# P transposed two chunks at a time, output stored two chunks at a time, and the ninth tokens moved in fewer transfers

## The chip, the cores and the metric

The kernel runs on one core of one Trainium2 chip. The metric is the device time of one execution in microseconds, lower is better. A core has five engines that run beside each other and wait for each other through semaphores: TensorE (PE in the profile, its weight loads are PEld), VectorE (DVE), ScalarE (ACT), GpSimd (POOL) and SyncE (SP), which does no arithmetic here and issues the DMA transfers. The inputs lie in the memory of the chip, are brought into the on-chip memory (128 partitions) by DMA, and TensorE writes its results into PSUM, from which DVE and ACT read.

## What is computed

Attention with a threshold over 8 batches, 8 heads, 576 tokens and 64 features a head, and behind it a feed-forward block with a maximum over three hidden layers:

```python
scores = scale * np.matmul(q, k.transpose(0, 1, 3, 2))
thresh = np.max(scores, axis=-1, keepdims=True) - tau
scores = np.where(scores >= thresh, scores, -1000000000.0)
scores = scores - np.max(scores, axis=-1, keepdims=True)
attn = np.exp(scores)
attn = attn / (np.sum(attn, axis=-1, keepdims=True) + 1e-09)
attn_out = np.matmul(attn, v)
x = attn_out.transpose(0, 2, 1, 3).reshape(B * S, H * D)      # 4608 x 512
h = np.maximum(np.maximum(x @ w1, x @ w2), x @ w3)            # 4608 x 768
out = h @ w_out                                               # 4608 x 512
```

## The kernel before

A "quad" is four heads of one batch, so there are 16 quads, two to a batch. Inside a quad the four heads are two couples, numbered r = 0 and 1, each of two heads, i = 0 and 1. The 576 tokens of a head are taken as 64 rows of nine tokens. Tokens 0 to 7 of each row make four blocks of 128 tokens; the last tokens of the 64 rows, the "ninth tokens", are a half block of 64. A quad has nine **chunks** of 128 query rows: four of i = 0 (numbers 0 to 3), one made of the ninth tokens of both i (number 4), four of i = 1 (numbers 5 to 8). There are 144 chunks in all.

For each chunk and each r TensorE makes a score tile of 128x576 in PSUM (`scores`), DVE takes its maximum (`maximum`), and the threshold and the exponentials are done in one of two ways, chosen by the table `MASKED`: by two passes on ACT, or by one on ACT and one on DVE (`exponents`, `numerators`). DVE takes the reciprocals of the sums for both r at once, and POOL multiplies and writes bf16 (`normalized`, lines 391 to 398): P, 128 x 1152, the two r beside each other. SP issues a transposing DMA (`turned`, lines 400 to 404) that writes P transposed into the tile `ptq` of the quad: nine blocks of 128 keys, and in each the columns of the chunk. There are six buffers for P (`PBUFS = 6`), so POOL can write P of chunk n only when the transfer of chunk n - 6 has landed.

When a quad is through, TensorE multiplies ptq with v (`product`), DVE and ACT copy the result to `xt`; with both quads of a batch done come the hidden layers (18 pieces a batch, `hid`), whose maximum is written to a tile `hT` of the batch (two buffers), and then the output: two pieces of two chunks each (`outp`) and one for the ninth tokens (`ninth`). ACT copies each output chunk from PSUM into a tile `ob` (four buffers) and SP stores it; the ninth tokens of a batch go out by two transfers. Batch 7 is split in two parts.

Loads, per quad: q and k (512 KB each), the ninth tokens of q and of k (64 KB each), v in two transfers, and the ninth tokens of v in two (`load`, lines 185 to 237). POOL casts v to bf16 (`cast_v`). All loads but three, all transposes and all stores but one are issued by SP.

The order is written out by hand in the string `ORDER`, one letter for each step, and `issue` carries it out. An engine does its steps in the order of the string. A capital is TensorE work and is followed by the number of the PSUM slot it writes (four slots of two banks): S a score tile, T the transposing of q and k on TensorE, O a product with v, F and B the two halves of a hidden or output piece, N a ninth piece. m, s, e, n, k and r are the steps of the softmax, p is half a P (POOL), t a transposing DMA (SP), l a load (SP), o and i stores (SP), y the casts of v, q a copy that swaps halves (POOL), and a, c, h, v, u, x, w and j are copies out of PSUM by ACT or DVE.

Before the first load lands, TensorE gets 12 transposes of the identity (`WARM = 12`, lines 607 to 609).

Every instruction of the kernel is recorded at line 93, a helper that keeps the order, so the profile's groups are told apart by tile names, not by lines.

Of the kernel before, what the change touches and what calls it, by code (L numbers as in the profile page):

```python
# [31 lines left out]
WARM = 12  # L32
# [3 lines left out]
PBUFS = 6  # L36
# [4 lines left out]
lllllllgllT0laclT1qqS0lacllzlqqS1mS2mS3lekS0lmlT1emlemalT2qclqkS1ylS3mgrlennemayS0elpcrS3nmpS1lnmplS2emT3gqq  # L41
esmtpS1erkT2paT0slceS3lpaT2ntS0cyqemS2ynrmtmqmqleenkS2plnS3resT1pmeS0qtmnpnpemzrteS2eznT3mpS0rcepaS3mytnqS1m
pT2lerapS3mgnS0plS2nqlermtpnmS3pntpermpS1mptekqT0mS2teeenkqnS3mrepmS1zcS0pmertenepS2mnpT1nmS3trS2mpS0enpmleg
yrmnplkeplS3ktS2eeknS0arrmptnS1mpmptS3mpS2eeremeS0ptmnS1ymnperkeptS3mT2encpS1lnsyO0mtqnmerkpgelnO2wqlnkpllS3
xrrreS0mptS2mnpT1maptesS2peS3pmteT1S0mpnS2cyS3lmO1lrmptmS0qewO2qennesrmepkS1epxkS3emF2nF0zmBkBpgT3ehnrF1vS2a
psS0nmzF3emBpgBesrrvS0tphS2mepF3mnT1plT0sBctapS2nvyF1nS0rsmtyT3eBzmeS2vpgS0mlpS1mF2lyennsqsmF0etBqrceBkpF1ht
S3snsvBnprF2vleS0pmBnpF1mhS3zsesrS0mS2epgmBntpF3ssvnF0qrBeqlF1evlzBemtBpS3hS2pnmS0tnrmO3pnmplnrsF2svgzeF0weB
pgS1evtyS3emBpS2nmtS1hkT3O0rakptmS3xrpsmS2ntpsS0smeF1pmT3etBqmnF2zvT0BtaczS1nvS3erlsmS2peS0lmpeS1mF3etmessF2
knlknlBkelresrmpS0npBmuptussrS1puS3umpS0lemS2lqeT1mtO3qnmqnssO0lpwelrncplS2xS1ptmeF0eF3mS2nokBetmF1hBrkpF2es
rBvnBpsevS3ytS0hmpS1emS2yepF3meF0trsmBpeBsvpnS2lnF1ymlT3nBvytaF2kT0hBkeF1lsrrecF3pBnvqBkF0phS2veS3mnptBmnpT2  # L50
F1sassrrlS3vpeS2lmepBlmF0eyoyS3vnoS2mnpBtsS1mphF3meT0tS2cF1ernsmBptS0esvpF2esmBqeS3lvqS0ntmqT1eBmyaF3rkF0hpB
nkS2nrsS1rvnBpmS3eptmO2pressmnptN1vepS3sweS0ptmjS2npmF1ekteT0knBrmpnssceT3yS2pasrrS0mqtuS3umpS2nmS0qleS1mlqe
S3ssmpS2oeO0ponmepmO1etqmerkO3pntkxrwS2xS0plmS3plmS1F2lpeeessmlnktT0eF3meBsscnlklnBkF0luF1rhktpBurBevF2pelS3
vpS0nlmByelmT1S3hlpsrsS0atmS2pnrS1mpeF3mtF0pemBnqF2ssvtnT1yBpecBqnrtS3vpnS1mS0hpmeF3tsmS1eBssrmepS0lrS2nvylF
1pemF3lyemBlBnskpoF2hsvT0oeBsprtS3avS1pnmF0eqS2tmF3epmBeqrS1stsvepS2mBepF0mlhT1nBkoO3nvtescS2nwT1nmF0F3akT2n
sBrrcpnBvS1phS2rmpetF3mepS0S1espmtS2epmBeF0rssmptT1eBkpaN2knO1snvjqtvS3xS2ermpS1nsS3rpmnS0mpteF2mpemqlnT1S3c
qnlS0rsqtmeS1BpmepmS0ektF1eemnklO3erslpulO0ynwlpnrklyS3xtrBskupermS0upS2umF3ptemS1pnS0mBnplsmS2hplF1meT3lBak
lF2ersqS3ovS0ntmpS1emBpeF3ssstvF0eBmeS2ktBhkF1nF3vniBmeBrF0sevpS2hrrspS1mnS3ptmeS2pmeF1qBstmeBpvnF2psS3snlrv
BylnmT1tS0hcpS3nmS2yepoF1rmeF0pomBeplF3ssvnBtyynBvT1hS2klaT0F3ssectqS1meS0qBrempT2eO1pmestaO0wnsrkpS2xvS1nF0
rpmnF3mptnBBsrpevS1phtS2meF0qsrS3mnpS1nmF2ptemBpT3esvT1qBtacS0eqS1rveqN3smepS2mnS0psmjS1ntmT2nF3cerlmpeS0klS  # L60
1peS2oknBlmnlrsmepO0lsuspkteO1uwelrS3kxlpS0emtF1empmF2oBktenekBkuS3hrsrS0pmuF2peS1smnpS3tmF0nysBmpeT1ryrtBsv
ayF3evS1pnS2mS0pemBpteS1mF2hpssmS0elF3emBlekBlF0nskF1tnsrBvpBhvyS2lpnvS0nqtS3rmepF1mF2eplBsmeBtrnrvS3pT0hmqF
1lnT2cBaT3knF0qvF2eBsqrceS1pvnBS3pstrmhS0pemS2nS1pmlF3nplsmF0eopBmS2oespsvS1ntBmeT3mO2atknsrsseF1vpS3terwpBn
mS0pS2hirmqS3nmS1qetF0smpF2nBpmetBpveS1S3rsempS0tnvpO1nsrmptesmS2peS3mxtF0meknT1oknS3S2lrecpBemyplermS1putS3
meF2ysmulykT1plN3akelO0kljesosO1weqtknqS3nrS0mleBpoxpmleT3S1cuF0nsorrF3mpnBtkpBhsS1uvS0lepS2meF3ymplF1eBsmle
BtsveS2F0hmF3nktBnT2kF1arBsvpnBrpveS0S2hptmS3nprF1smeS0plmF2nyisBmeF3vpBelsrBrqtvT1hT0qcS2epS3tmnS1ymapS2nsm
lS3peF0tsmpF1esmF2nBlrspnBrsovBnqtS3vhpS0empS2leF1mpS3lemBtnrmF0pF2nsvpBetsT3vBeS1rcepF0tkhO3ynmynrS2wnT1pmB
apT3tsssesT2cqN1avqeS3rS2jpmeF0pmtS1eBqnmS2qnsvS3S1qemS0pnmF2ntrkpesT3smBepmnrtcS1puS0umpS3erS2mtpeS1mpF0nsm
ekS3nS2meBkemnO1rupupmO3txskeO2ewtkS1rrpS3mS0pmptexnF2S1essmeBpmeF3F0tshkF1nrkS2peBlmBnlyssBvpF2ihvyF3eBssro
eS0pvBoepmO2teyvS0S1sremptF3wmpS0nS2nmoBmS1ihS0rmepF3tnF2pmBnkF0noBsrvpnBtS1vphS3sesmF0teF2mBerBpveS3ynF1yvp  # L70
F0nmS2tnBmBessF3khF2errvBpeBpvO0nkptO3hkN1wxsS2jeS0pmeS1tmF2srF3mepBrespBveS1ptS0vnpS2mnF3tnmrmF1peskepBerkn
ptBupoO2tO0xuO2wukuN3xrF1npF2hprF0vF1ptvF2hF0jpvF1vF2thF0vF1vF2hiF0vF1vF2ihF0vF1vF2ohF0voO1voO2wF0xF2F1hF3vF
2vF1hF3vF2vF1hF3vF2vF1hF3vF2vF1hF3vF2vF1hF3vBvF3uuoBoN0ufojdi
# [31 lines left out]
def kernel(  # L105
# [39 lines left out]
    wo = one.tile([128, NF, DM], BF16, name="wo")  # L145

# [38 lines left out]
    def load(g, first=False):  # L185
        b, qd = quads[g]
        L = Ls[g] = dict(b=b, qd=qd, first=first)
        for n in "qk":

            L[n] = ld.tile([128, 20, D], F32, name=n + "m")  # L190
        L["vm"] = ld.tile([128, 4, 4, D], F32, name="vm")
        L["vr"] = ld.tile([128, 2, D], F32, name="vr")

        def rows_of(src):
            return src[b, 4 * qd:4 * qd + 4].rearrange("(r i) (p c) d -> (i p) r c d", r=2, c=9)

        def both(n, src, rows, i=None):

            t = L[n].rearrange("p (r c) d -> p r c d", r=2)[rows, :, 0:8]
            return t, one_of(src, i)[:, :, 0:8] if i is not None else rows_of(src)[:, :, 0:8]  # L200
# [4 lines left out]
        if first:  # L205
            for i in range(2):
                put = [(n, src, half(n, i), nc.scalar if n == "k" and i == 0 else sync) for n, src in (("k", k), ("q", q))]
                for n, src, rows, e in put:
                    e.dma_start(out=L[n][rows, 8:10], in_=one_of(src, i)[:, :, 8])
                    yield  # L210
# [4 lines left out]
                for n, src, rows, e in put:  # L215
                    if i == 0:
                        e.dma_start(out=L[n][rows, 10:18], in_=one_of(src, i)[:, 1, 0:8])
# [24 lines left out]
    def cast_v(L):  # L242
# [4 lines left out]
        for r in range(2):  # L247
            rows = slice(64 * r, 64 * r + 64)
            pool.tensor_copy(out=L["vrb"][rows, 2 * r:2 * r + 2], in_=L["vr"][rows])
            yield  # L250
# [6 lines left out]
    def couple(L, n, r, j, rows=slice(0, 128)):  # L257

        f = 8 if j == 4 else 10 * r + (0, 4, 2, 6)[j]
        return L[n][rows, f:f + 2, :].rearrange("p a d -> p (a d)")  # L260
# [25 lines left out]
    def transposed(L, r, n=None, i=None):  # L286
# [16 lines left out]

        def done(m, heads, banks):
# [61 lines left out]
    def threshold(c, r):  # L366
        th = c["th", r] = small.tile([128, 1], F32, name="th")
# [354 lines left out]
    x = 0  # L722
# [39 lines left out]
```

## Time and profile before

| | |
|---|---|
| median of three runs | 448.61 us (448.44 to 449.05) |
| the profiled execution's own time | 448.81 us |
| its span on the core | 447.0 us |
| PE, ACT, DVE, POOL busy | 427.8, 404.5, 391.4, 310.7 us |
| transposing DMAs | 144, each 1.39 us of issue on SP (median), 4.6 us from issue to landing |
| stores of `ob` | 32 of 256 KB, 31 of them by SP |
| stores of the ninth tokens (`obr`) | 16 of 64 KB |
| loads of ninth tokens of v (`vr`) | 32 of 32 KB |
| loads of ninth tokens of q and k, quads 1 to 15 | 30 of 64 KB |

The profile is one execution, 1.8 us shorter by its span than by its device time. A group's line names the tile written and the tiles read, the shapes, how many there were, the busy time, the mean time of one, and the idle time of the engine just before them with what ended it. The chain is followed back from the last instruction, at each step to what released it. The row PEclk is the clock that TensorE was granted, in tenths of full speed. A busy TensorE is not one at its peak, since the ends of matmuls are modelled.

### The profile page before, as it was taken

Reading aid. Unit: us, or ns where it says so; the run is one execution under the profiler, and the core shown is the slowest. Engines: PE = TensorE matmul, PEld = TensorE weight load, DVE = VectorE, ACT = ScalarE, POOL = GpSimd, SP = SyncE. Lnnn points to the kernel's source line nnn. Section 1 sums busy time; section 2 is a strip of 40 time slices with the busy share of each in tenths; the row PEclk is TensorE's granted clock in tenths of the full one; section 3 lists DMA queues with packets and bytes.
Section 4 is the critical chain, followed back from the end, with each engine's and each line's share of the span. In section 5 each row is a group of like instructions: output and inputs, shape, how many; then the busy total and the mean of one; then the engine's idle time right before and its main releaser. Section 6 shows DMA issues by size and latency. Waiting matters only on the chain.

```text
span 447.0 us, 14312 instructions
## 1 busy us (share of the span) xinstructions
PE 427.8 (96%) x5188; PEld 320.1 (72%) x5188; DVE 391.4 (88%) x1225; ACT 404.5 (90%) x841; POOL 310.7 (70%) x420
## 2 busy tenths in 40 slices
PE   8777799999999999999999999999999999999995
PEld 6443545887787777788687776787688876786862
DVE  4988899989899999999899899999999998998542
ACT  3999999998999999999999999999999999898422
POOL 2799789998667875876767776687748784657200
PEclk9987789999999999999999999999999999999999
DMA  7999999999999999999989989989999996995812
GB/s 177 317 228 203 258 207 230 213 194 279 198 218 170 233 202 207 217 261 166 164 232 180 270 133 231 171 167 219 177 263 158 236 179 93 169 166 112 149 73 107
DMA packets 212840, 87.46 MB, mean 196 GB/s; under 512 B 185889, under 2 KB 199713, under 8 KB 212769
## 3 DMA queue, kind: packets, MB, share of 16 engines
q1 hardware_dynamic: 212320, 85.98, 96.2%
q8 instruction: 41, 0.67, 0.6%
q10 hardware_dynamic: 448, 0.56, 0.4%
q14 instruction: 31, 0.25, 0.2%
HBM read 34.60 MB, written 9.44 MB: 99 GB/s over the span
## 4 chain that ended last, share of the span: by engine, by line
PE 84%; ACT 5%; DVE 3%; POOL 3%; DMA 1%; issue 1%; SPq 1%; DVEq 0%; POOLq 0%
PE ph L93 32%; PE sc L93 30%; PE po L93 10%; PE o L93 9%; ACT z L93 4%; PE tp L93 3%; DVE z L93 2%; POOL P L93 2%; DMA qm<-in_q_dram 1%; SPq L93 1%; POOL qs L93 1%; DVE kt L93 0%; ACT qt L93 0%; POOL vb L93 0%; DVE stage L93 0%
## 5 line engine op out<-in xcount | busy, mean ns | idle before, releaser
L93 POOL TENSOR_SCALAR P<-z,rs 128x576 bf16<-128x576 f32 x250 | 197.8, 803 | 71.6 <-DVE rs L93 37.0
L93 DVE TENSOR_SCALAR_CACHE_REDUCE z<-sc 128x576 f32<-128x576 f32 x250 | 182.0, 752 | 19.8 <-PE sc L93 11.1
L93 PE MATMUL sc<-kt,qt 64*128 64x320 f32 (+2 forms) x640 | 184.0, 442 | 5.6 <-DVE z L93 3.2
L93 PE MATMUL sc<-kt,qs 64*128 64x256 f32 (+2 forms) x640 | 183.1, 430 | 6.2 <-ACT z L93 2.8
L93 PE MATMUL ph<-xt,w 64*128 64x288 bf16 (+2 forms) x2160 | 164.4, 283 | 0.0
L93 PEld LDWEIGHTS <-w 64*128 64x128 bf16 (+1 forms) x2160 | 127.0, 94 | 27.0 <-issue 4.2
L93 PEld LDWEIGHTS sc<-kt,qs 64*128 64x128 f32 (+1 forms) x640 | 95.7, 183 | 30.5 <-ACT z L93 7.5
L93 ACT ACTIVATE z<-z 128x576 f32<-128x576 f32 x170 | 114.6, 678 | 0.1
L93 PEld LDWEIGHTS sc<-kt,qt 64*128 64x128 f32 (+1 forms) x640 | 95.5, 183 | 20.9 <-DVE z L93 6.7
L93 ACT ACTIVATE z<-z,th 128x576 f32<-128x576 f32 x134 | 99.8, 769 | 2.3 <-DVE rs L93 1.5
L93 DVE SCALAR_TENSOR_TENSOR z<-z 128x576 f32<-128x576 f32 x80 | 62.9, 801 | 0.3 <-ACT z L93 0.3
L93 POOL COPY qs<-qt 64x640 f32<-64x640 f32 (+3 forms) x66 | 45.6, 691 | 14.5 <-ACT qt L93 11.1
L93 ACT ACTIVATE z<-z,nm 128x576 f32<-128x576 f32 x71 | 53.5, 767 | 0.0
L93 PE MATMUL po<-wo,hT 64*128 64x512 bf16 (+1 forms) x480 | 53.2, 356 | 0.1
L93 ACT ACTIVATE hm<-ph 128x576 bf16<-128x576 f32 (+2 forms) x54 | 31.8, 590 | 14.9 <-PE ph L93 14.6
L93 DVE TENSOR_TENSOR hm<-ph,hm 128x576 bf16<-128x576 f32 (+2 forms) x54 | 37.0, 686 | 9.4 <-PE ph L93 8.7
L93 POOL TENSOR_SCALAR P<-stage,rs 128x576 bf16<-128x576 f32 x38 | 29.9, 793 | 18.2 <-DVE rs L93 7.5
L93 PEld LDWEIGHTS <-hT 64*128 64x128 bf16 (+1 forms) x480 | 28.8, 97 | 17.0 <-issue 2.1
L93 DVE TENSOR_TENSOR hT<-ph,hm 128x576 bf16<-128x576 f32 (+2 forms) x54 | 37.1, 687 | 3.8 <-PE ph L93 1.3
L93 PE MATMUL o<-ptq,vb 128*64 128x64 bf16 (+2 forms) x544 | 38.6, 282 | 0.0
L93 ACT ACTIVATE z<-sc,nm 128x576 f32<-128x576 f32 x45 | 32.1, 746 | 4.3 <-DVE z L93 4.2
L93 ACT ACTIVATION_READ_ACCUMULATOR z<-z 128x1 f32 x170 | 33.4, 197 | 0.0
(42 smaller groups left out, 410.7 us busy)
## 6 DMA issues: line engine op xcount, KB each, us to landing
vm<-in_v_dram SPq DMA_DIRECT2D x32, 256.0 KB, 5.3
out_dram<-ob SPq DMA_DIRECT2D x31, 256.0 KB, 4.3
qm<-in_q_dram SPq DMA_DIRECT2D x15, 512.0 KB, 4.5
km<-in_k_dram SPq DMA_DIRECT2D x15, 512.0 KB, 5.3
stage<-in_moe_w_dram SPq DMA_DIRECT2D x9, 512.0 KB, 4.8
ptq<-P SPq DMA_TRANSPOSE x144, 4.6
stage<-in_moe_w_out_dram SPq DMA_DIRECT2D x3, 512.0 KB, 5.3
vr<-in_v_dram SPq DMA_DIRECT2D x32, 32.0 KB, 2.9
```

Source lines behind the costliest of these rows:

```text
L93: ins = fn(*a, **kw)
```

## The change

- P of two neighbouring chunks of a quad (`place`) lies in one tile of 128 x 2 x 1152, of which there are three, and one DMA transposes both. A quad has nine chunks, so the last goes alone; so do those of the last quad (`JOINED = 15`) and one chunk of quad 14. `ptq` is laid out chunk by chunk, so that a product reads runs of 128 columns instead of one run.
- Output pieces take the chunks 0 and 2, and 1 and 3, and each piece is stored by one DMA from one tile of two chunks, with two such tiles instead of four single ones. Batch 7 still stores each chunk.
- The ninth tokens of q and k are loaded once for a batch, into tiles of their own; the ninth tokens of v come with all eight heads by two transfers a batch into one tile without a second buffer.
- `hT` is one tile of two batches. In batches 1, 3 and 5 the ninth tokens are put first, so that they lie next to those of the batch before, and one piece (`ninths_of_two`) makes the output of both, copied once and stored once. Batches 6 and 7 keep a piece each.
- The work on TensorE before the first load is 36 bf16 matmuls on a tile of zeros, and two more stand behind the first transposes.
- `ORDER` is written anew. The sequence of S, T and O is the same; t has 84 entries for 144, l 104 for 134, o 17 for 31, i 5 for 8, N 5 for 8. `th` has five buffers for six.

```diff
-WARM = 12
+WARM = 36
-PBUFS = 6
+PBUFS = 3
+JOINED = 15
...
     def load(g, first=False):
...
-            L[n] = ld.tile([128, 20, D], F32, name=n + "m")
+            L[n] = ld.tile([128, 16, D], F32, name=n + "m")
+            L[n + "8"] = ld.tile([128, 4, D], F32, name=n + "8") if qd == 0 else Ls[g - 1][n + "8"]
...
-            for n, src in (("q", q), ("k", k)):
-                sync.dma_start(out=L[n][:, 8:10], in_=rows_of(src)[:, :, 8])
-                yield
+            if b == 0 or qd == 0:
+                mine = slice(2 * qd, 2 * qd + 2) if b == 0 else slice(0, 4)
+                for n, src in (("q", q), ("k", k)):
+                    sync.dma_start(out=L[n + "8"][:, mine], in_=rows_of(src)[:, mine, 8])
+                    yield
...
-        for r in range(2):
-            sync.dma_start(out=L["vr"][64 * r:64 * r + 64],
-                           in_=v[b, 4 * qd:4 * qd + 4].rearrange("h (p c) d -> p c h d", c=9)[:, 8, 2 * r:2 * r + 2, :])
-            yield
-
+        if qd == 0:
+            L["vr"] = ld.tile([128, H, D], F32, name="vr", bufs=1)
+            for r in range(2):
+                sync.dma_start(out=L["vr"][64 * r:64 * r + 64],
+                               in_=v[b].rearrange("h (p c) d -> p c h d", c=9)[:, 8])
+                yield
...
     def transposed(L, r, n=None, i=None):
...
+            if i == 0 and r == 0:
+                warmed(2)
...
     def normalized(c):
-        c["P"] = P = pp.tile([128, W], BF16, name="P")
+
+        at, full = place(c)
+        if at == 0:
+            c["P2"] = pp.tile([128, 2, W], BF16, name="P")
+        else:
+            c["P2"] = made[c["n"] - 1]["P2"]
+        P = c["P2"][:, at]
         for n in range(2):
             pool.tensor_scalar(out=P[:, n * S:(n + 1) * S], in0=c["z", n],
                                     scalar1=c["rs"][:, n:n + 1], scalar2=1.0, op0=OP.mult, op1=OP.mult)
-            if n:
-                line["t"].append(c)
+            if n and full:
+                line["t"].append((c, at + 1))
             yield
 
-    def turned(c):
+    def turned(c, n):
         L = Ls[c["g"]]
         if "pt" not in L:
-            L["pt"] = pt_pool.tile([128, 9, W], BF16, name="ptq")
-        sync.dma_start_transpose(out=L["pt"][:, :, c["idx"] * 128:(c["idx"] + 1) * 128], in_=c["P"])
+            L["pt"] = pt_pool.tile([128, 9, 9, 128], BF16, name="ptq")
+        x = c["idx"]
+        sync.dma_start_transpose(out=L["pt"][:, x + 1 - n:x + 1].rearrange("p c j u -> p (c j) u"),
+                                 in_=c["P2"][:, 0:n].rearrange("p c w -> p (c w)"))
...
+                    u = min(n, 128)
+                    tensor.matmul(ps[64 * i:64 * i + 64, p0:p0 + n].rearrange("p (a u) -> p a u", u=u), w,
+                                  pt[:, q0[i] // 128:(q0[i] + n + 127) // 128, 4 if m == 4 else m + 5 * r,
+                                     q0[i] % 128:q0[i] % 128 + u],
                                   start=(m == 0), stop=(m == 4))
...
-                ob = hp_.tile([128, DM], F32, name="ob", bufs=4)
+                if a == 0:
+                    my["ob"] = hp_.tile([128, 2, DM], F32, name="ob")
+                both = my["ob"]
+                ob = both[:, a]
...
-                stores.append(lambda: sync.dma_start(out=rows_out[:, (0, 2, 1, 3)[c + a]:8:4], in_=ob))
+                if part is not None:
+                    stores.append(lambda: sync.dma_start(out=rows_out[:, (0, 2, 1, 3)[c + a]:8:4], in_=ob))
+                elif a == 1:
+                    stores.append(lambda: sync.dma_start(
+                        out=rows_out[:, 0:8].rearrange("p (x s a) m -> p x s (a m)", x=2, a=2)[:, :, c],
+                        in_=both.rearrange("p a m -> p (a m)")))
...
+        def ninths_of_two():
+
+            my = {}
+
+            def first(where):
+                my["ps"] = ps = bank("po", where)
+                h = halves([[(ps[:, 512 * a:512 * a + 256],
+                              lambda rows, f=f: h_of(b)[rows, f, 512:640],
+                              lambda rows, a=a, f=f: wo[rows, f, 256 * a:256 * a + 256]) for f in range(NF)] for a in range(2)])
+                h[0]()
+                h[1]()
+
+            def done():
+                ob = hp_.tile([128, DM], F32, name="ob9", bufs=1)
+                scalar.activation(out=ob.rearrange("p (a u) -> p a u", a=2),
+                                  in_=my["ps"].rearrange("p (a u) -> p a u", a=2)[:, :, :256], func=AF.Copy)
+                stores9.append(lambda: sync.dma_start(
+                    out=out[(b - 1) * S:(b + 1) * S, :].rearrange("(x p c) m -> x p c m", x=2, c=9)[:, :, 8],
+                    in_=ob))
...
+    def place(c):
+
+        n = c["n"]
+        if c["g"] >= JOINED:
+            return 0, True
+        here = lambda m: 0 <= m < len(steps) and steps[m] == (c["g"], c["idx"] + m - n)
+        before = 0
+        while here(n - before - 1):
+            before += 1
+        return before % 2, before % 2 == 1 or not here(n + 1)
...
-    for t in vrs:
+    plain = vrs[2].rearrange("p h d -> p (h d)")[:, 0:128]
+    vector.memset(vrs[2], 0.0)
+    for t in vrs[0:2]:
         for x in range(2):
             vector.memset(t[64 - 64 * x:128 - 64 * x, 2 * x:2 * x + 2, :], 0.0)
-    warm = bank("warm", 3)
-    for _ in range(WARM):
-        tensor.transpose(warm[:, 0:128], identf, identf)
+
+    def warmed(n, where=3):
+
+        warm = bank("warm", where)
+        for _ in range(n):
+            tensor.matmul(warm[:, 0:128], plain, plain, start=True, stop=True)
+    warmed(WARM)
```

More of the change, by code (lines that the diff above doesn't have):

```diff
@@ L45 @@
[L45 to L49, printed above, removed]
@@ L74 @@
+F1vF2hF3vF1vF2hF3vF1vF2hF3vF1vF2hF3vBvF3uuoBoN0ufojdi
 """
@@ L470, in ffn @@
         mine = [c for c in (part or range(5)) if c < 4]
-        chunks = [tuple(mine[c:c + 2]) for c in range(0, len(mine), 2)] + ([4] if part is None or 4 in part else [])
+        gap = 2 if part is None else 1
+        chunks = ([(0, 2), (1, 3)] if part is None else [tuple(mine[c:c + 2]) for c in range(0, len(mine), 2)]) + ([4] if part is None or 4 in part else [])
         st = {}
@@ L567, in ffn @@
         return ([hid(f, wi) for f in range(NF) for wi in range(3)],
-                [outp(c) for c in chunks if c != 4], [ninth() for c in chunks if c == 4])
+                [outp(c) for c in chunks if c != 4],
+                [ninths_of_two() if ninth_first(b) else ninth() for c in chunks if c == 4 and not ninth_first(b + 1)])
     quads = [(b, qd) for b in range(B) for qd in range(H // 4)]
```

124 lines of the change are left out of this document (69 added, 55 removed).

## The prediction, made before the changed kernel was run

> **What bounds the kernel now.** I read the page first: its shares, its slices and its chain.
>
> ```profile
> PE 427.8 (96%) x5188; PEld 320.1 (72%) x5188; DVE 391.4 (88%) x1225; ACT 404.5 (90%) x841; POOL 310.7 (70%) x420
> ...
> PE   8777799999999999999999999999999999999995
> ...
> ACT  3999999998999999999999999999999999898422
> ...
> PEclk9987789999999999999999999999999999999999
> ...
> PE 84%; ACT 5%; DVE 3%; POOL 3%; DMA 1%; issue 1%; SPq 1%; DVEq 0%; POOLq 0%
> ```
>
> TensorE is full from the seventh slice on and carries 84% of the chain. The first 60 us are another stage: there TensorE has gaps and a reduced clock. So I asked for busy times by stretch.
>
> ```profile
> 16.00:20.00 4.00, 3.67 (x49) 2.26 (x49) 3.89 (x15) 4.00 (x10) 3.80 (x7) 1.00 1.08 323
> 20.00:30.00 10.00, 7.32 (x60) 4.35 (x56) 8.06 (x25) 10.00 (x22) 9.43 (x13) 0.83 1.14 270
> 30.00:40.00 10.00, 6.78 (x63) 3.85 (x60) 7.67 (x23) 10.00 (x23) 9.69 (x14) 0.97 1.01 155
> 40.00:50.00 10.00, 9.67 (x54) 6.10 (x52) 7.73 (x23) 9.57 (x23) 8.75 (x12) 0.52 1.15 249
> 50.00:60.00 10.00, 7.44 (x37) 3.69 (x36) 9.74 (x32) 9.19 (x20) 8.49 (x10) 0.83 1.09 272
> 60.00:68.00 8.00, 6.62 (x86) 3.31 (x82) 7.43 (x23) 7.97 (x20) 6.80 (x10) 1.00 0.99 188
> ...
> 100.00:150.00 50.00, 50.00 (x663) 40.29 (x662) 47.21 (x154) 48.16 (x99) 36.40 (x50) 1.00 1.07 217
> ```
>
> The columns are length, then PE, PEld, DVE, ACT and POOL busy with their counts, clock, DMA share, GB/s. From 16 to 68 us ACT is idle 52.0 - 50.7 = 1.3 us and POOL 5.0 us: the start is bound by ACT, with POOL close behind it. From 100 us on TensorE is never idle, ACT is at 96% and more, and POOL has 27% to spare. Last, the waits from 13 to 68 us (who waited for whom: us, times, longest), and the users of `ptq` over the whole span.
>
> ```profile
> DVE z L93 <- PE sc L93: 3.1, 6, 1.0
> ...
> DVE z L93 <- POOL P L93: 2.9, 5, 1.0
> ...
> ACT z L93 <- DVE z L93: 1.2, 2, 0.8
> ```
>
> ```profile
> L93 SPq DMA_TRANSPOSE ptq<-P x144: 1244/1386/4057, 19.4 to 419.7; - x144
> ...
>   PEld L93: 0.5, 1
> ...
> DMA to landing us min/median/max: 3.2/4.6/8.1
> ```
>
> Waits for transposed P cost TensorE 0.5 us, once. POOL waits for no DMA on its way to P. So the transfers, however busy their queue, are hidden; what the change makes cheaper is not what the end waits for. The span is 447.0 us in an execution of 448.81 us; the sum is made against that, 0.2 us above the median of 448.61.
>
> **The transposes.** 60 pairs and 24 singles take the place of 144. SP issues 60 instructions fewer. If a pair is issued in the time of one, SP saves 60 x 1.39 = 83 us, if it takes two, nothing. Either lies in SP's waits (121 us of them are for POOL's P), so the end gets 0. The DMA's bytes are the same. A pair lands later than a single: at least the median single, 4.6 us, at most two in series, 9.2 us. I take 4.6 + 1.4 = 6.0 us, one more issue, since the nearest row, transposes issued back to back, has an issue as its pitch. If the cover goes, `product` waits for it. The last chunk of a quad goes alone, as before, and the order gives it about the same distance to its product. In the trace the tightest place is quad 9: its last P ended at 264.5, its product began at 269.51, so 5.0 us less 4.6 leaves 0.4 us. A pair still being issued ahead of that single would use it up; its issue is over by then, one chunk being 2.9 us (35 chunks of P from 100 to 200 us). I take 0, bound -0.5 (the present wait goes) and +5 (five quads with under 5 us, 1 us each).
>
> **The three double buffers of P.** This is a new wait. With nine chunks a quad the ring is tightest where a single stands in it: chunk 9 reuses the buffer of 4 and 5. At the start a chunk takes 2.5 us of time (19 halves in 24 us) and its two halves 1.5 us, so from the end of 5 to the begin of 9 it is 4 x 2.5 - 1.5 = 8.5 us. Before, six buffers gave 6 x 2.5 - 1.5 = 13.5 us. The transfer needs some 1 us until SP comes to it and 6.0 us to land: 7 of 8.5 us. At 9.2 us it would be 1.7 us late. Queued behind a waiting POOL are the copies of `qs` for the scores, the casts, and the next P, which free `z` for DVE. I take 0; the bounds are 0 and the slow rival below.
>
> **SP's other transfers.** 30 loads, 14 stores of `ob` and 9 of ninths go, 53 x 0.6 us = 32 us of issue, all in SP's slack. The v ninths carry twice the bytes by whole eight heads to both halves (128 KB for 32 KB in half as many transfers; 2 MB in all for 1 MB of 87 MB). Their single buffer makes SP wait for POOL's casts of the batch before; queued behind are transposes. The new order casts quad 1's ninths at the fifteenth score tile and loads the next only at the 25th. Cost 0, +1 if SP stalls. The pair of output chunks waits for the second copy, one ACT copy of 0.59 us later, with no reader: 0.
>
> **Ninths.** TensorE has the same columns: two batches had 2 x 6 pairs of 256, now 12 pairs of 256, with one stop between its halves, some 0.1 us three times. ACT had eight copies of 372 ns, 2.98 us; now two of these and three of 512 columns at the 591 ns of `ob`, 2.52 us. That is 0.46 us less on an engine at 96 to 99% in the middle, but TensorE ends there: I take -0.2 for both, between +0.3 and -0.5. `th` with five buffers instead of six: 145 ns writes, read by the next ACT pass; 0.
>
> **The products' layout.** The reads of ptq go in runs of 128. Nothing in the trace reads bf16 in this way. The nearest row is contiguous, 4 x 512 columns as good as at the pitch of `ph` (16 matmuls in 0.98 us). Bound: 0, and 10% of the chain's 9% for `o`, 4 us. I take 0, as the strided output of `tp` keeps its pitch.
>
> **Before the first load.** Twelve transposes end at 4.2 us, and the first `tp` waits for its load until 4.85. A pair of `ph` of 288 columns takes 0.98 / 8 = 0.12 us at full clock, so 128 columns at half clock some 0.11 us (estimate), and 36 take 3.9 us, to about 5.0 us. The first `tp` is then 0.1 to 0.2 us late. What it buys shows in two lines of the timeline:
>
> ```profile
> 8.69 0.74 PE L93 MATMUL sc<-kt,qt 64*128 64x320 f32 x1
> ...
> 14.10 0.43 PE L93 MATMUL sc<-kt,qt 64*128 64x320 f32 x1
> ```
>
> Up to 12 us the scores run at about half speed, although the clock's row says 1.00 there, so the transposes had not opened the clock. The Trainium skill, page "TensorE: Matmul & The Clock Gate", part 4, says that transposes do not count as activity; the trace agrees by 0.74 against 0.43 us. By that rule the term below is its -0.2; were real matmuls no better than transposes, it would be +0.2. With real matmuls the scores of 6.6 to 11.8 us may take half. But the chain stands on the load of q, which lands at 12.0, then on ACT. ACT's idle time before 12.7 is filled with nothing that was ready; DVE gains up to 0.7 us. On the path I take -0.2, between +0.2 and -0.7.
>
> **The start behind it.** Its order on TensorE, ACT and DVE is almost letter for letter the same, with POOL's casts moved by a few steps. The chain has 4.1 us of `sc` at half clock between 40.4 and 46.2 us and 0.9 us at 59.5. What full clock there, or a DVE that runs ahead, could give is bounded by ACT's waits of 1.2 us from 13 to 68. I take -0.9: the moved POOL work and the earlier start shift the gaps that led to the slow stretches, with no proof that they go. Its other end is the slow clock elsewhere, +1.5.
>
> **Sum.** 448.8 - 0.2 (ninths) - 0.2 (first scores) - 0.9 (start) = 447.5 us.
>
> **Rivals.** *Nothing comes through* (18%): ACT keeps its order, and the start stays: 448.4, within 447.7 and 449.5. *More comes through* (10%): ACT's second passes, which take 0.70 to 0.72 us from 20 to 35 us and 0.67 later, lose that too: 25 of them with their 0.04 us longer readouts make 2 us: 447.5 - 2.0 = 445.5. *The ring of P makes it slower* (22%): place, POOL from 16 to 68 us. It decides from a landing of 7.5 us; a single already took up to 8.1. At 9.2 + 1 us a wait is 1.7 us, and four to six reuses before the first hidden layer make 7 to 10 us, less POOL's 5.0 us: +2 to +5 on the sum without the start's gain, 448.4, in the middle 451.9. Against it: the median single leaves 3 us. *Products late* (7%): 1 us in each of three tight quads, 447.5 + 3 = 450.5. *The clock closes again* (6%): scores that end by 9.5 us leave TensorE idle until 12.1. In the trace 1.96 us of idleness before 25.37 stand ahead of a clock of 0.50 at 26 to 28 us. Then the scores of 13.7 to 17 us take twice, about 3 us more for TensorE, of which ACT's lead of some 1.5 us covers half: 448.4 + 1.5 = 449.9. The same page's rule in "Why this matters for your kernels" is no idle gaps over about 3 us; this gap would be just under it.
>
> **Numbers.** The forecast has 37%, own range 446.3 to 447.7. Faster by over 0.2% (0.9 us, about what can be told from no change): 37 + 10 = 47%. Within it: 18%. Slower: 22 + 7 + 6 = 35%. The range 444.8 to 452.0 leaves out half of the ring's cases (11%) and little below.
>
> **What would show it.** The first hidden piece, begun at 76.3 us, should come up to 1.3 us earlier and everything behind it by the same. The first scores at 6.6 us should be 0.43 us long. A row "POOL P <- DMA ptq" would show the ring, "PEld <- DMA ptq" above 0.5 us late products, a longer `o` than 282 ns the layout, and a changed landing time the price of a pair. I am wrong if SP's queue was holding something that no wait shows, or if a pair takes over 7.5 us.

## The result, and the profile after

The changed kernel takes 468.39 us (median of four runs, 465.88 to 470.38); the kernel before takes 448.83 us beside it (448.44 to 449.25). The ratio is 1.0419, with a 95% interval of 1.0384 to 1.0455. The profiled execution took 469.64 us, its span is 467.9 us. The forecast was 447.5 us, within 444.8 and 452.0.

From the page of the kernel after: the shares, the slices and the chain.

```profile
PE 435.8 (93%) x5214; PEld 319.2 (68%) x5214; DVE 392.2 (84%) x1224; ACT 405.7 (87%) x838; POOL 309.7 (66%) x420
...
PE   7868879898699998999999999999999999999996
...
PEclk9876899999799999999999999999999999999999
...
PE 70%; POOL 7%; DVE 6%; DMA 5%; ACT 5%; issue 3%; SPq 2%; POOLq 0%; DVEq 0%; ACTq 0%
```

TensorE is busy 8.0 us longer than before, and the clock's row is lower; no other engine is busy for over 1.2 us more. What is new is idleness: the row PE has gaps in its eighth, tenth and eleventh slices, and the chain holds 14 points less of TensorE and more POOL, DVE and DMA. Busy times by stretch, first of the kernel after, then of the one before, say where (length, then PE, PEld, DVE, ACT, POOL, clock, DMA share, GB/s):

```profile
75.00:100.00 25.00, 22.09 (x302) 17.58 (x300) 21.65 (x67) 22.03 (x47) 19.57 (x25) 1.00 0.80 179
100.00:125.00 25.00, 19.76 (x231) 13.24 (x226) 16.45 (x48) 16.83 (x35) 16.56 (x22) 0.88 1.08 223
```

```profile
75.00:100.00 25.00, 24.98 (x344) 20.28 (x342) 22.87 (x71) 24.97 (x54) 24.20 (x30) 1.00 1.05 209
100.00:125.00 25.00, 25.00 (x307) 19.63 (x304) 23.35 (x80) 23.50 (x49) 18.90 (x25) 1.00 1.07 229
```

Before, TensorE was hardly idle from 75 to 125 us (0.02 us); now it is idle for 50 - 41.85 = 8.15 us, and ACT, DVE and POOL with it. The waits of the kernel after (who for whom: us, times, longest), and below them the one row of the two that the kernel before has:

```profile
DVE z L93 <- POOL P L93: 22.3, 25, 4.1
...
POOL P L93 <- DMA ptq<-P: 14.5, 6, 4.2
```

```profile
DVE z L93 <- POOL P L93: 6.9, 14, 1.0
```

POOL cannot write P until a transfer has landed, and DVE cannot take its maximum until POOL has freed `z`. The transposes themselves, and SP's own waits (`stage` is the tile in which weights land before POOL casts them):

```profile
L93 SPq DMA_TRANSPOSE ptq<-P x84: 1241/2710/7197, 21.6 to 440.6; - x84
...
DMA to landing us min/median/max: 3.2/5.2/10.2
```

```profile
SPq L93 <- POOL vr L93: 32.4, 8, 6.3
...
SPq L93 <- POOL w L93: 12.4, 4, 5.1
```

Taken apart by size, a pair takes 3.32 us of issue and lands 5.69 us after it began (medians of 60). SP waited for `vr` 12.0 us before and for `w` 6.1.

To see at which place time is lost I used one more reading of the traces: the start of maximum k of DVE's 288 (k counts from 0), less the start of the same one in the kernel before. All kernels have them in the same order, so the lag grows exactly where a kernel loses. These are the steps that count (us; the labels are those of the experiments below):

| k (time before) | after | e2 | e10 | e1 | e7 | e5 | e9 | e12 |
|---|---|---|---|---|---|---|---|---|
| 52 (72.4) | 0.6 | 1.4 | -0.3 | 1.9 | 1.0 | 1.1 | 1.7 | 0.6 |
| 84 (117.8) | 12.3 | 7.7 | -0.3 | 4.0 | 2.2 | 1.1 | 1.7 | 0.6 |
| 116 (164.1) | 13.2 | 7.7 | -0.3 | 5.1 | 2.8 | 1.1 | 1.9 | 0.8 |
| 124 (172.8) | 15.7 | 7.7 | -0.3 | 7.6 | 2.8 | 1.0 | 1.9 | 0.8 |
| 132 (184.2) | 18.4 | 7.7 | -0.3 | 10.3 | 5.5 | 3.4 | 1.9 | 2.2 |
| 204 (285.6) | 20.1 | 7.8 | -0.2 | 12.2 | 6.6 | 5.6 | 1.9 | 3.5 |
| 276 (390.2) | 21.6 | 8.0 | -0.2 | 13.6 | 7.9 | 7.3 | 2.8 | 4.4 |
| end of span | 20.8 | 9.5 | -0.1 | 13.1 | 7.9 | 7.3 | 2.7 | 3.8 |

The kernel after loses 11.7 us between the 52nd and the 84th maximum, 2.5 us up to the 124th, 2.7 us up to the 132nd, and some 1.6 us at each of two places more. The experiments give most of this its cause. Each column is one execution, and executions of one kernel differ by up to 4.6 us (465.88 to 470.38 us after; 448.02 to 452.65 us before, beside e12). So a lag of under 2 us that is there from the start says nothing.

### The profile page after: what moved, and what is told of

Same layout as the page of the kernel before. It is cut to its first block, busy times and chain, and to the rows that moved or that the text cites. A ratio compares the mean times of both kernels' runs of the same rounds, so it can differ in the third digit from the quotient of the medians.

```text
span 467.9 us, 14128 instructions
## 1 busy us (share of the span) xinstructions
PE 435.8 (93%) x5214; PEld 319.2 (68%) x5214; DVE 392.2 (84%) x1224; ACT 405.7 (87%) x838; POOL 309.7 (66%) x420
## 4 chain that ended last, share of the span: by engine, by line
PE 70%; POOL 7%; DVE 6%; DMA 5%; ACT 5%; issue 3%; SPq 2%; POOLq 0%; DVEq 0%; ACTq 0%
PE ph L93 27%; PE sc L93 25%; PE po L93 8%; PE o L93 7%; ACT z L93 4%; DMA ptq<-P 4%; DVE z L93 4%; POOL P L93 4%; PE tp L93 3%; SPq L93 2%; POOL qs L93 2%; DMA qm<-in_q_dram 1%; POOL vb L93 1%; DVE stage L93 1%; POOL vr L93 1%
## 5 line engine op out<-in xcount | busy, mean ns | idle before, releaser
L93 POOL TENSOR_SCALAR P<-z,rs 128x576 bf16<-128x576 f32 x250 | 195.0, 793 | 92.5 <-DVE rs L93 44.2
L93 DVE TENSOR_SCALAR_CACHE_REDUCE z<-sc 128x576 f32<-128x576 f32 x250 | 182.3, 752 | 35.5 <-POOL P L93 22.3
L93 PE MATMUL sc<-kt,qs 64*128 64x256 f32 (+2 forms) x640 | 185.9, 435 | 7.1 <-ACT z L93 4.5
L93 PE MATMUL sc<-kt,qt 64*128 64x320 f32 (+2 forms) x640 | 187.0, 447 | 5.8 <-DVE z L93 2.1
L93 PE MATMUL ph<-xt,w 64*128 64x288 bf16 (+2 forms) x2160 | 165.4, 284 | 3.7 <-DVE z L93 3.1
L93 PEld LDWEIGHTS <-w 64*128 64x128 bf16 (+1 forms) x2160 | 126.3, 94 | 32.2 <-issue 8.6
L93 PEld LDWEIGHTS sc<-kt,qs 64*128 64x128 f32 (+1 forms) x640 | 95.2, 184 | 33.6 <-ACT z L93 8.8
L93 ACT ACTIVATE z<-z 128x576 f32<-128x576 f32 x170 | 114.3, 675 | 0.1
L93 PEld LDWEIGHTS sc<-kt,qt 64*128 64x128 f32 (+1 forms) x640 | 95.0, 184 | 23.8 <-ACT z L93 5.8
L93 ACT ACTIVATE z<-z,th 128x576 f32<-128x576 f32 x134 | 99.6, 767 | 6.3 <-DVE th L93 4.3
L93 DVE SCALAR_TENSOR_TENSOR z<-z 128x576 f32<-128x576 f32 x80 | 63.1, 803 | 0.4 <-ACT z L93 0.3
L93 POOL COPY qs<-qt 64x640 f32<-64x640 f32 (+3 forms) x66 | 45.8, 694 | 13.8 <-ACT qt L93 10.4
L93 PE MATMUL po<-wo,hT 64*128 64x512 bf16 (+2 forms) x480 | 53.1, 355 | 0.5 <-DVE z L93 0.2
L93 ACT ACTIVATE z<-z,nm 128x576 f32<-128x576 f32 x71 | 53.3, 765 | 0.0
L93 ACT ACTIVATE hm<-ph 128x576 bf16<-128x576 f32 (+2 forms) x54 | 31.8, 589 | 18.0 <-PE ph L93 17.7
L93 DVE TENSOR_TENSOR hm<-ph,hm 128x576 bf16<-128x576 f32 (+2 forms) x54 | 37.0, 685 | 11.7 <-PE ph L93 10.9
L93 POOL TENSOR_SCALAR P<-stage,rs 128x576 bf16<-128x576 f32 x38 | 30.4, 806 | 20.3 <-DVE rs L93 8.3
L93 PE MATMUL o<-ptq,vb 128*64 128x512 bf16 (+2 forms) x544 | 39.1, 282 | 2.4 <-DVE z L93 1.9
L93 PEld LDWEIGHTS <-hT 64*128 64x128 bf16 (+1 forms) x480 | 28.3, 95 | 18.6 <-issue 2.5
L93 DVE TENSOR_TENSOR hT<-ph,hm 128x576 bf16<-128x576 f32 (+2 forms) x54 | 37.1, 686 | 3.8 <-PE ph L93 1.3
L93 ACT ACTIVATE z<-sc,nm 128x576 f32<-128x576 f32 x45 | 32.0, 737 | 3.9 <-DVE z L93 3.8
L93 PEld LDWEIGHTS <-vb 128*64 128x64 bf16 x544 | 22.9, 111 | 17.0 <-issue 8.9
```

What stands on the lines that cost most here:

```text
L93: ins = fn(*a, **kw)
```

## The experiments

The theories in the order in which they came. **R**: three double buffers are too short a ring for P. **Q**: SP, which works in order, is late with the transposes because it stands in loads. **O**: the other parts cost. **C**: of these, the new order's early casts of v. **D**: or the parts themselves, in any order. **N**: of these, the ninth piece for two batches.

**e1, the change without the pairs.** Six single buffers and a transpose for each chunk, in the new order.

```diff
-PBUFS = 3
+PBUFS = 6
-            c["P2"] = pp.tile([128, 2, W], BF16, name="P")
+        c["P"] = P = pp.tile([128, W], BF16, name="P")
```

> The changed kernel with the pairs alone undone: each chunk has its own transfer and one of six single buffers for P, the first of each former pair is transposed before the next chunk's P is written; all else as changed. Theory R (the ring of three double buffers is too short: POOL waits 14.5 us for transfers and DVE 22.3 us for POOL): 447.5 to 450, POOL waits for no transfer. Theory Q (SP stands in order behind loads that wait for POOL's casts, 32.4 us on the casts of v's ninths for 12.0 before, because that tile has one buffer; transfers are late whatever their size): 458 to 468. Theory O (the other parts: the layout of the products, the stores, the work before the first load): 465 to 469.

461.83 us against 449.92 beside it, ratio 1.0255 [1.0227, 1.0283]. R missed; the time lies in Q's range. Without the pairs 6.6 us of the loss go (468.39 less 461.83, or 7.7 with each kernel against the one before beside it), and a second cause of about 12 us stands beside them.

**e2, the kernel before with the pairs alone.** Three double buffers, `place`, `turned` and the products' layout of the change, nothing else; in the order one of two t is left out.

```diff
-PBUFS = 6
+PBUFS = 3
+JOINED = 15
-            pt[:, 4 if m == 4 else m + 5 * r, q0[i]:q0[i] + n],
+            pt[:, q0[i] // 128:(q0[i] + n + 127) // 128, 4 if m == 4 else m + 5 * r, ...],
```

> The kernel before with the pairs alone: one transfer for two chunks, three double buffers, the layout of the transposed tile that goes with it; loads, stores, ninths and the work before the first load as before, the same order less the transfers that fall away. Theory R: 462 to 470. Theory Q: 449 to 455, since the loads of v's ninths have their two buffers. Theory O: 448 to 450.

459.53 us against 449.92, ratio 1.0209 [1.0184, 1.0234]: R's mechanism, at a price under the one it gave, and above what Q and O gave. The pairs alone lose 7.7 us by the 84th maximum, and hardly anything behind it but 1.6 us at the 277th, where POOL waits 3.5 us for a transfer once more. Its row "POOL P L94 <- DMA ptq<-P" has 11.0 us in six waits.

**e3, pairs in the buffers, but two transfers for each at the same place.**

```diff
-        sync.dma_start_transpose(out=L["pt"][:, x + 1 - n:x + 1]..., in_=c["P2"][:, 0:n]...)
+        for k in range(n):
+            sync.dma_start_transpose(out=L["pt"][:, x + 1 - n + k], in_=c["P2"][:, k])
```

> The changed kernel, with each pair sent by two transfers, one behind the other at the same place in the order, from the same double buffer. Theory R: 465 to 470, since a buffer is free no earlier. If the length of one transfer is what costs (3.3 us of issue, 5.7 us to landing by the median): under 460. Theory Q: 465 to 470.

467.64 us, ratio 1.0385 [1.0344, 1.0425], the same as the change within its spread, where R and Q both had it. Whether the DMA is one or two makes no difference that can be told; what is left of the pair is that its buffer comes free only as a whole. (The trace of e3 loses 6.7 us by the 84th maximum, that of the kernel after 12.3. The two executions, 465.40 and 469.64 us, lie near opposite ends of their kernels' spreads, so at this place the table's columns are good to some 6 us.)

**e4, the kernel before with four buffers for P instead of six**, with single transposes.

```diff
-PBUFS = 6
+PBUFS = 4
```

> The kernel before with four single buffers for P instead of six, nothing else. A pair's ring lets the first chunk of a pair be written after the transfer of the chunk three to five back has landed; four singles give four back always. Theory R: 455 to 466, with POOL waiting for transfers 5 to 12 us. Theory Q: 448.5 to 451.

464.27 us, ratio 1.031 [1.0277, 1.0342]. With no pair at all, a short ring loses 10.3 us between the 52nd and the 84th maximum (lag 2.7, then 13.0), at the same place. "POOL P L93 <- DMA ptq<-P" has 13.0 us, a little above R's 5 to 12. So it is the ring. Q missed in e2 (449 to 455) and here (448.5 to 451).

What is at that place? Lines of SP's timeline in the kernel after, and below them three of POOL's (start, us, engine, transfer or operation; in brackets the idle time before and what ended it):

```profile
79.97 3.29 SPq L93 DMA_DIRECT2D stage<-in_moe_w_dram  x2
83.31 1.91 SPq L93 DMA_DIRECT2D vm<-in_v_dram  x1
85.26 3.52 SPq L93 DMA_TRANSPOSE ptq<-P  x1
...
102.53 5.33 SPq L93 DMA_TRANSPOSE ptq<-P  x1
...
110.32 13.43 SPq L93 DMA_TRANSPOSE ptq<-P  x4
```

```profile
90.94 1.46 POOL L93 TENSOR_SCALAR P<-z,rs 128x576 bf16<-128x576 f32 x2 [3.49 <-DMA ptq<-P]
...
99.96 1.46 POOL L93 TENSOR_SCALAR P<-z,rs 128x576 bf16<-128x576 f32 x2
...
119.73 1.47 POOL L93 TENSOR_SCALAR P<-z,rs 128x576 bf16<-128x576 f32 x2 [4.22 <-DMA ptq<-P]
```

SP stands at loads into `stage` until POOL has cast the weights that lie there (row "SPq <- POOL w" above), then at v, and only then issues a pair. POOL meanwhile waits for that transposing DMA, and its next casts wait behind the P that it cannot write. The longest way is that of the pair whose P ends at 101.42 us: SP is then at loads and at the pair ahead of it (5.33 us from 102.53), issues it at 110.32, and it lands at 119.58; POOL's next P has waited 4.22 us for it. The chain of waits has "85.26 5.50 DMA ptq<-P" and "110.32 9.26 DMA ptq<-P" in this stretch. The kernel before stands at the same two loads for the same 3.29 us, and six buffers cover it:

```profile
77.74 3.29 SPq L93 DMA_DIRECT2D stage<-in_moe_w_dram  x2
```

So the delay that Q speaks of is how R comes about, not its rival; the tile of v's ninths that Q blamed has its two buffers in e2 and e4, and they lose time all the same.

**e5, all parts but the pairs, in the order of before.** The three double ninth pieces and their stores stand where the new order has them, since their buffer asks for it; the letters of what the parts leave out are gone, and the ninth tokens of v have a letter of their own, behind the casts of the batch before. At one such place the string reads:

```diff
-nlklnBkF0luF1
+nlklnBN0kF0luF1j
```

> The changed kernel without pairs (six single buffers), all other parts as changed, but in the order of the kernel before: its letters for P, casts of v, transposes, loads and stores, less those that fall away; the ninth pieces of batches 1, 3 and 5 where the new order has them, the loads of v's ninths behind the casts of the batch before. Theory C (the new order puts POOL's casts of v for every second quad ahead of P's, where they wait for TensorE's products while those wait for POOL; 11 us of the 12 us that stayed without pairs): 448 to 451. Theory D (the parts themselves: one buffer for v's ninths, stores by two, ninth pieces): 456 to 462. Theory Q as in the first experiment: 456 to 462.

456.36 us against 450.32, ratio 1.014 [1.0116, 1.0164]: at the low end of the range that D and Q share and far from C's. Going back to the old order gains 5.5 us against e1 (5.9 with each against the kernel before beside it), so C has a part of it; 6.0 us stay.

**e6, the whole change in the order of before**: e5 with the pairs.

```diff
-PBUFS = 6
+PBUFS = 3
+JOINED = 15
```

> As the one before, but with the pairs and three double buffers: the whole change, in the order of the kernel before. Theory R for the pairs with C for the rest: 457 to 461, as the pairs alone gave 459.5. If the new order was there to make the pairs cheaper: 465 or more.

464.5 us, ratio 1.0327 [1.0295, 1.0358], in neither range. The pairs cost 8.1 us on top of e5, 9.6 on the kernel before (e2) and 7.7 in the new order (the change less e1): a loss of like size whichever order stands around it. R and C together had been given less, since neither knew of the 6 us of e5.

**e7, e1 with only the casts of v back at their old places**: each letter y stands behind as many steps of TensorE as before, and the ninth tokens of v are loaded behind them. One of the places:

```diff
-O2nmeO0eyyytppmqtmO1
+O2nmeO0etppmqtmO1
```

> The changed kernel without pairs in its new order (461.8), with one thing put back: POOL's casts of v stand where the kernel before has them, by the count of TensorE's pieces, and the load of v's ninths behind those of the batch before. Theory C: 449 to 453. If something else in the new order costs: 457 to 462.

458.16 us, ratio 1.0176 [1.0148, 1.0204]: 3.7 us less than e1 (4.1 with each against the kernel before beside it), in the range for something else, and not all of C's gain. The casts are one part of it. In the trace of e1 one such place, first POOL, then DVE behind it:

```profile
173.65 1.04 POOL L94 CAST vb<-vm 128x1024 bf16<-128x1024 f32 x1 [0.90 <-PE o L94]
```

```profile
176.16 0.76 DVE L94 TENSOR_SCALAR_CACHE_REDUCE z<-sc 128x576 f32<-128x576 f32 x1 [2.61 <-POOL P L94]
```

The cast wants the buffer of `vb` that products still read, waits 0.90 us, and takes 1.62 us with the two casts of `vr` behind it; the two P behind it are late, and DVE stands 2.61 us. This is the step at the 124th maximum, 5.1 to 7.6 us in e1, which e7 doesn't have (2.8 and 2.8). In the kernel after the same wait of DVE is 2.59 us, at 184.22 us. A second such place stands at 75.46 us of the kernel after: a cast of `vb` and two of `vr`, 2.67 us, stand there ahead of P, and the lag grows by 1.6 us in the kernel after, e1 and e3, and not in e5, e6 and e7. The two steps are 2.6 + 1.6 = 4.2 us in e1, which is the price of the casts.

**e8, pairs with four double buffers, on the kernel before.** Room comes from two `hm` instead of three and from single buffers for the ninth rows of q and of k.

```diff
-PBUFS = 3
+PBUFS = 4
-            L[n] = ld.tile([128, 20, D], F32, name=n + "m")
+            L[n] = ld.tile([128, 16, D], F32, name=n + "m")
+            L[n + "8"] = ld.tile([128, 2, D], F32, name=n + "8", bufs=1)
-                    st["hm", f] = hp_.tile([128, nr, n], BF16, name="hm", bufs=3)
+                    st["hm", f] = hp_.tile([128, nr, n], BF16, name="hm", bufs=2)
```

> The kernel before with the pairs alone (459.5), and four double buffers instead of three; room is made by two buffers instead of three for the first hidden maxima and one instead of two for the ninth tokens of q and k. Theory R: 449 to 452, and POOL waits under 2 us for transfers. If the length of a pair's transfer costs by itself, or the room taken costs: 455 to 460.

459.86 us, ratio 1.0211 [1.0186, 1.0235]: by its time a miss for R, and POOL waits 5.5 us for transfers where R gave under 2. The lag says otherwise: it is -0.5 us at the 84th and 0.3 at the 172nd maximum, and then steps at one place, to 10.6 at the 180th; 4.4 of the 5.5 us are waited there. There SP waits up to 10.0 us for TensorE ("SPq L94 <- PE tp L94: 17.6, 8, 10.0"): the load of the ninth rows of k needs the single buffer that I had taken, and transposes queue behind it. The loss was my own.

**e10, the same with a single buffer for q's ninth rows alone.**

```diff
-            L[n + "8"] = ld.tile([128, 2, D], F32, name=n + "8", bufs=1)
+            L[n + "8"] = ld.tile([128, 2, D], F32, name=n + "8", bufs=1 if n == "q" else 2)
```

> Before with the pairs alone, four double buffers of P (no more P in flight than eight chunks), room made by two buffers of the hidden layer's half instead of three and one buffer instead of two for the ninth rows of q alone. Theory R (the ring of P is what the pairs lose by, and the 10 us step of the last such kernel was the single buffer for the ninth rows of k): 448.5 to 451.5 us, no step of 2 us or more in the lag. Rival Q (pairs as such cost, since SP is held 3.3 us by each): 455 to 460 us, with the loss spread over the run.

449.42 us against 450.31, ratio 0.999 [0.9968, 1.0011]. With four double buffers the pairs cost nothing and gain nothing that can be told; the Q of this expectation, that a pair costs by itself, falls. Its trace, DVE's waits for P and the transposes:

```profile
DVE z L94 <- POOL P L94: 5.5, 13, 0.9
```

```profile
L94 SPq DMA_TRANSPOSE ptq<-P x84: 1267/2777/6496, 24.1 to 419.4; - x84
...
DMA to landing us min/median/max: 3.2/5.2/10.6
```

The transposes are as slow as in the kernel after (5.2 us median for all, up to 10.6), and yet nothing waits for them: DVE's waits for P are back at 5.5 us, and the row "POOL P <- DMA ptq" is gone. That settles R for the pairs; the whole change with four double buffers was not tried.

**e9, e5 with one ninth piece per batch at the places of before.**

```diff
 def ninth_first(b):
-        return b % 2 == 1 and b not in SPLIT
+        return False
```

> The kernel of the order of before with all other parts but the pairs (456.4 us, 7.3 us behind), with one more thing put back: each batch's ninth tokens go through a matmul piece, an eviction and a store of their own, at the places of before. Theory N (the piece for two batches holds ScalarE's eviction and then TensorE's next FFN piece, some 2.2 us at each of three places): three steps go, 449.0 to 451.0 us, and the lag of VectorE's maxima does not step at the 128th, the 204th and the 276th. Theory D (the rest, that is the loads once per batch, the stores of two chunks and the warm matmuls, costs it): 454.5 to 457 us, the steps stay.

450.39 us against 450.31, ratio 0.9996 [0.9972, 1.002]. N holds, D falls: the 6 us of e5 are the ninth pieces, and everything that is left (fewer loads, one buffer for v's ninths, stores of two chunks, five `th`, the warm-up) costs and gains nothing clear of the interval's 1.3 us. The three steps are gone from the lag. N put the cost down to ACT's copy out of PSUM; e12 shows that this is only part of it.

**e12, is it the place or the size of the piece?** As e9, with the ninth pieces of batches 1, 3 and 5 alone moved to the places of the double ones.

```diff
-nlklnBkF0luF1
+nlklnBN0kF0luF1j
```

> The kernel with every part but the pairs, in the order of before, ninth tokens by one piece per batch (450.4 us, no step in the lag where its pieces stood at the places of before). Now the pieces of the second, fourth and sixth batch alone are moved to the three places at which the change puts the piece for two batches; there they are 12 matmuls of 64x256 pairs instead of 24 (some 0.86 us instead of 1.71) and an eviction of 0.37 us instead of 0.38 for twice the rows. Theory S (what costs is TensorE's time in one block while VectorE has run dry behind it, so the price goes with the size of the piece): steps of 0.9 to 1.4 us at the 128th, 204th and 276th maximum, 452.5 to 454.5 us. Theory L (the place costs, whatever the size): steps of 2 us, 455.5 to 457.5 us. Theory Z (neither by itself): no step, 449.5 to 451 us.

452.59 us against 449.98, ratio 1.0065 [1.0035, 1.0095]. Half a piece makes steps of 1.4, 1.3 and 1.2 us, where the double one of e5 made 2.4, 2.3 and 2.0: theory S. (In e5 and in e12 the piece and the hidden piece after it share a PSUM slot at this place, and 0.69 and 0.48 us of the first step are the wait for ACT's eviction; in the kernel after they don't share one, and the step is 2.7 us all the same.) Two lines of TensorE and one of DVE in the kernel after show the mechanism:

```profile
193.82 1.73 PE L93 MATMUL po<-wo,hT 64*128 64x256 bf16 x24
195.38 2.61 PE L93 MATMUL ph<-xt,w 64*128 64x288 bf16 x40
```

```profile
197.12 0.76 DVE L93 TENSOR_TENSOR hm<-ph,hm 128x576 bf16<-128x576 f32 x1 [2.67 <-PE ph L93]
```

The new place is right behind the batch's last output piece. Those pieces give DVE nothing to do; with 1.73 us more of them DVE runs dry until the next hidden piece. At the old places (e9) the same columns stand among score tiles and no such wait follows. The new place isn't free to choose: the one `hT` of two batches is written again by the next.

**e11, the kernel before with the new warm-up alone.**

```diff
-WARM = 12
+WARM = 36
-        tensor.transpose(warm[:, 0:128], identf, identf)
+            tensor.matmul(warm[:, 0:128], plain, plain, start=True, stop=True)
```

> Before with the warm-up changed alone: 36 matmuls of bf16 instead of 12 transposes ahead, two more behind each early transposing piece. Theory: the start is worth 2 us at most in either direction, 448.0 to 450.8 us, all of it in the first 25 us of the lag. If the start is a cause by itself: 452 us or more.

450.32 us against 450.31, ratio 1.0005 [0.9984, 1.0027]. It costs and gains nothing that can be told.

**The sum**, by medians, each kernel less the kernel before beside it. Those medians run from 448.83 to 450.32 us, so a term is good to about 1 us. The pairs cost 7.7 us in the new order (the change less e1), 8.1 in the order of before (e6 less e5) and 9.6 alone (e2). The new order costs 5.9 us (e1 less e5), of which the casts are 4.1 (e1 less e7). The ninth pieces cost 6.0 (e5 less e9), the rest 0.1 (e9). With the pairs as e6 has them that is 8.1 + 5.9 + 6.0 + 0.1 = 20.1 us, where 468.39 - 448.83 = 19.6 us were lost. No version tried beats the kernel before by more than the interval.

## Why the prediction was wrong

- **What bounds the kernel** was read rightly: TensorE, full from 60 us on, and transfers that hardly anything waits for. The conclusion, that they stay hidden under the change, was not. What hid them was six buffers, and the change halved the ring's steps in the same stroke.
- **The transposes**: a pair estimated at 6.0 us to landing measured 5.69 us (median; 14 of the 60 took over 7.5 us, the sign of being wrong that the prediction named, up to 10.2). SP saves nothing by it, as one of the two cases had it (3.32 us of issue for a pair, 1.39 for a single). Right.
- **The three double buffers, taken as 0**: the step that failed. Its sum was "some 1 us until SP comes to it and 6.0 us to land: 7 of 8.5 us". The 6.0 was right in the median; the 1 us was not. From the end of P to the issue of its transpose the kernel before already takes 2.58 us in the median and up to 9.87; after, it is up to 8.89, and the longest way from P to landed is 18.15 us (15.97 before). Between 76 and 118 us POOL began 28 halves of P in the kernel before, 3.0 us a chunk, so by the prediction's own formula the ring covers 4 x 3.0 - 1.5 = 10.5 us there. The median way, 5.75 us, would have passed; the tail decides, and the tail is what SP does in order ahead of the transpose, and landings of up to 10.2 us. I had written SP's waits down as slack, 121 us of them for POOL's P, without asking for the longest stretch between a finished P and its transpose.
- **The rival "the ring of P"** (22%) had the mechanism, and the row that would show it ("POOL P <- DMA ptq") is there, 14.5 us. Its place was wrong (16 to 68 us; it is 80 to 118) and with it its price: 2 to 5 us where the pairs cost 8 to 10. It was looked for where chunks are densest, not where SP's queue holds loads that wait for POOL.
- **SP's other transfers**: 0, or +1 for the single buffer of `vr`. The rest of the change without order, pairs and ninth pieces costs 0.1 us in e9, so 0 was right for these alone. SP's wait for `vr` did grow from 12.0 to 32.4 us in the kernel after (18.0 in e3, whose median is the same within its spread); what of that adds to the ring's delay was not tried apart.
- **Ninths, -0.2 with a bound of +0.3**: wrong by the place. The columns were counted rightly; but where they are put, TensorE's 1.7 us in one block leave DVE dry, some 2 us at each of three places.
- **The start, -0.9, from "almost letter for letter the same" order**: wrong. The moved casts were named and then priced as a gain; they cost 4.1 us, at 75 and 182 us, where the prediction did not look at the order at all, and the new order with all in it 5.9. What the 1.8 us between them are stays open.
- **The products' layout, 0**: right; the mean of `o` is 282 ns in both kernels.
- **The first scores, -0.2**: from 6.76 us on a score takes 0.38 to 0.53 us, as forecast, but the first hidden piece starts 0.6 us later than before, not earlier. The rival "the clock closes again" (6%) did occur: in the kernel after the clock is 0.65 from 12 to 16 us (1.00 before), and the scores from 12.88 us on take 0.54 to 0.74 us (from 13.73 us on 0.38 to 0.53 before). It occurred in e11 and in e9 too, at no cost that the medians of these show. TensorE's timeline in e11, then two stretches (length, PE, PEld, DVE, ACT, POOL, clock, DMA share, GB/s):

```profile
11.95 0.25 PE L93 MATMUL tp<-identf,qm 64*128 64x64 f32 x1 [1.93 <-DMA qm<-in_q_dram]
...
13.53 0.90 PE L93 MATMUL sc<-kt,qt 64*128 64x320 f32 x1 [0.81 <-DVE kt L93]
```

```profile
12.00:16.00 4.00, 3.19 (x28) 2.46 (x30) 2.13 (x7) 3.46 (x9) 2.69 (x5) 0.59 1.08 339
16.00:20.00 4.00, 4.00 (x30) 2.08 (x29) 3.25 (x9) 3.20 (x7) 3.70 (x6) 0.56 0.91 266
```

The faster first scores end at 10.02 us, q lands at 11.95, transposes follow, and the next scores, at 13.53, are slow (0.90 us) at a clock of 0.59. In e8 the same wait is 1.98 us long and the scores behind it take 0.53 us. The Trainium skill, page "TensorE: Matmul & The Clock Gate", Part 1, says that a window of some 3.4 us without activity halves the clock, and that the window runs free of the kernel, so that its phase differs from run to run. In e11 10.02 to 13.53 us is 3.5 us without a matmul other than transposes, and the clock falls; that it stays up in e8, over 3.56 us without one (9.65 to 13.21), fits the free window. The clock records that the traces keep show the window: in all 14 kernels every stretch of one granted clock, but the last, which the end cuts off, is a whole multiple of 3.41 us, from a first record at 3.76 to 12.19 us. In e11 the clock falls at 12.69 us, so the window ahead begins at 9.28 and holds the last 0.74 us of scores: it need not be empty. In e8 an edge at 11.49 us cuts the same gap, and the two windows hold 1.57 and 1.24 us of scores. The prediction's reading of the clock's row is put right by this too: ahead of the first record the row says 1.00 for want of one. In the kernel before the first record, of full clock, stands at 12.09 us, and the slow scores end at 11.88.

## What to carry to other kernels

A ring of buffers is sized by the longest way from "written" to "free", not by the median: take from the trace the time from each producer's end to its transfer's issue, and look at what stands ahead of it on an in-order queue. Joining two transfers into one halves how many buffers can come free one by one; if the bytes stay the same and the issue time is no less, as here (3.32 us for two, 1.39 for one), there is nothing to gain for that. And the place of a piece of work counts, not only its size: here blocks of 1.7 us for TensorE alone, put behind other such work, cost 1.4 to 2.7 us each, blocks of 0.85 us 1.2 to 1.4, and the same columns among score tiles nothing.

## What the runs showed of the hardware

One transposing DMA of 128 x 2304 bf16 takes SP 3.32 us of issue in the median (2.41 at least), more than two of 128 x 1152 (1.39 each, 1.24 at least), so its issue time goes with the bytes; landing takes 5.69 us against 4.6 for the single in the kernel before. The prediction had left both cases open.

In the 14 traces the clock that TensorE is granted changes only at steps of 3.41 us, and where the steps fall differs from execution to execution. So neither way of filling the time before the first load fixes the clock that follows. Behind twelve transposes the first scores took 0.63 to 0.90 us in the kernel before and 0.38 to 0.53 us in e8, which has the same twelve: there full clock is granted from 4.66 us on, and in the 3.41 us ahead of it TensorE had done nothing but the twelve transposes, 2.82 us of them. So in this execution the clock opened behind transposes alone, against the prediction's reading that they don't open it. Behind 36 bf16 matmuls full clock came by 6.7 us in eight of nine kernels; in e3 it came at 10.48 us, and the first scores took 0.63 to 0.90 us. These are single executions, and what share of a window opens the clock was not tried.
